# Load order, keys computed ahead and earlier weight sums at the start of a linear-attention and gated-MLP kernel

## The chip, the cores and the metric

One NeuronCore of one Trainium2 chip. The time is the device time of one execution in microseconds (us). Before the change: median 1449.56 us of three runs (1448.41 to 1450.8). TensorE (the matrix engine) is PE in the profiles, VectorE is DVE, ScalarE ACT, GpSimd POOL; a span is the profiled execution from its first to its last instruction.

## The reference, cut to what matters

```python
x = A_x                                   # 1 x 2048 x 1024, bf16
x = x + A(layernorm(x), wqkv, wo)         # linear attention, 32 heads of 32
x = x + B(layernorm(x), w_gate, w_up, w_down)
x = x + A(layernorm(x), wqkv, wo)
x = x + B(layernorm(x), w_gate, w_up, w_down)

def A(x, wqkv, wo):
    q, k, v = split(x @ wqkv)
    pq, pk = phi(q), phi(k)               # phi(t) = where(t > 0, t + 1, exp(t)) + 1e-6
    ...                                   # o = (pq . (pk^T v)) / (pq . sum(pk)), then @ wo
def B(x, ...):  return ((x @ w_gate) * (x @ w_up)) @ w_down
```

## The kernel before

The 2048 tokens are 16 tiles of 128. In the first attention layer a tile is normalised on VectorE and POOL (`start` makes its statistics, `b_one` normalises it), transposed on TensorE and copied by ScalarE (`step_t`), and projected: keys ("k") and queries ("q") in two halves of 512 columns, eight matmuls each. ScalarE and VectorE evacuate each half. Ten tiles are projected plainly. The other token pairs go through "quads", a seven-product scheme for two tiles, which needs sums of weight blocks (`tw_make`, each VectorE instruction over 2048 elements) and of token blocks (`s_make`). The program gives each engine its instructions in a fixed order; a helper adds the semaphores.

```python
NHOLD = 2; NPL1 = 10; LNX = (3, 5, 6)
...
if first:
    lnp.start(0); lnp.b_one()
    lnp.start(1); lnp.step_t(1)
    lnp.b_one();  lnp.start(2)
...
seq = [("k", i) for i in range(NHOLD)] if NPL else []
for i in range(NHOLD, NPL):
    seq += [("q", i - NHOLD), ("k", i)]          # k0 k1 q0 k2 q1 k3 ...
...
for kind, i in seq:
    for h in range(2):
        ev = proj(kind, tok[i], h)               # 8 matmuls
        ev()                                     # exp, relu, min, add
        if kind == "k":
            lnstep(i, h)                         # statistics, normalise; transpose
    if kind == "q" and i >= 1 and len(twk) > 1:
        twk.pop(0)()                             # one weight sum of the keys
    elif kind == "q" and i >= 1 and len(twq) > 1:
        twq.pop(0)()                             # one of the queries
...
for f in twk: f()                                # the last key sum, then the quads
```

The loads are issued in program order on one queue: tile 0, first half of the key weights, tile 1, second half, tile 2, and so on.

Of the kernel before, what the change touches and what calls it, by code (L numbers as in the profile page):

```python
# [180 lines left out]
def build_kernel(nc, A_x, A_wqkv, A_wo, B_w_gate, B_w_up, B_w_down, out):  # L181
    _, S, D = A_x.shape
    F = B_w_gate.shape[1]
    NST, NSB, KT, NG, NFT, NDH = S // 128, S // 512, D // 128, D // 128, F // 128, D // 512
# [8 lines left out]
    NHOLD = 2  # L193
# [128 lines left out]
    with ExitStack() as es:  # L322
# [85 lines left out]
        def r_x(i, lo=0, hi=D):  # L408
            return [(O_X + (i * D + lo) * 2, O_X + (i * D + hi) * 2)]
# [10 lines left out]
        def r_w(base, lo, hi):  # L420
            return _seg(base, KT, D * 2, lo * 2, hi * 2)

        def dma(dst_ap, src_ap, wr, key, rd=()):
            P.add("sp", lambda e: e.dma_start(dst_ap, src_ap), rd=rd, wr=wr, dma_sem=key)
# [218 lines left out]
        def load_w(n, c):  # L643
            t, v, c0, base = WSRC[n]
            dma(t[:, :, c * 512:(c + 1) * 512], v[:, :, c0 + c * 512:c0 + (c + 1) * 512], r_w(base, c * 512, (c + 1) * 512), KW[n][c])
# [28 lines left out]
        def tw_make(n, eng, parts):  # L674
            b11, b12, b21, b22 = [w_blk(n, kb, h) for kb in range(2) for h in range(2)]
            t1, t2, t3, t4 = [tw_blk(n, c) for c in (1, 2, 3, 4)]
            step = 4 // parts
            ops = []
            for o, a, b in ((t1, b12, b11), (t2, b22, t1), (t4, b21, t2), (t3, b22, b12)):
                for k in range(0, 4, step):  # L680
                    def one(o=o, a=a, b=b, k=k):
                        P.add(eng, lambda e: e.tensor_tensor(out=o[0][:, k:k + step], in0=a[0][:, k:k + step], in1=b[0][:, k:k + step], op=ALU.subtract),
                              rd=rsub(a[1], k, step) + rsub(b[1], k, step), wr=rsub(o[1], k, step))
                    ops.append(one)
            return ops
# [33 lines left out]
        def pack():  # L719
            u = pk_n[0]  # L720
            if u >= NU:
                return
            pk_n[0] += 1
            assert RG.get("n", 0) <= u, (RG["n"], u)
            j, m = unit_jm(u)
            w16 = wscr[u].bitcast(BF16)[:, 0:2048].rearrange("p (i k c) -> p i k c", i=2, c=128)
            for i in range(2):
                c0 = j * 256 + (1 - i) * 128
                dma(w16[:, i], wgu_v[m][:, :, c0:c0 + 128], R(V_PK + u * 64 + 32 * i, 32), KPK[u])
# [124 lines left out]
        def s_make(tok, p):  # L854
            a11, a12 = x_blk(tok[2 * p], 0), x_blk(tok[2 * p], 1)
            a21, a22 = x_blk(tok[2 * p + 1], 0), x_blk(tok[2 * p + 1], 1)
            s1, s2, s3, s4 = [s_blk(tok, p, c) for c in (1, 2, 3, 4)]
            return [(lambda o=o, x=x, y=y, op=op: tt(o[0], x[0], y[0], op, x[1] + y[1], o[1]))
                    for o, x, y, op in ((s1, a21, a22, ALU.add), (s2, s1, a11, ALU.subtract),
                                        (s3, a11, a21, ALU.subtract), (s4, a12, s2, ALU.subtract))]  # L860

        def layer_A(lnp, nxt, first):
# [21 lines left out]
            def proj(kind, i, h):  # L884
                t, v, c0, base = WSRC[kind]
                bank = B_KQ[kq_i[0] % len(B_KQ)]
                kq_i[0] += 1

                def fn(e):
                    return [e.matmul(psb(bank), xnT[:, k, i * 128:(i + 1) * 128], t[:, k, h * 512:(h + 1) * 512],  # L890
                                     start=(k == 0), stop=(k == KT - 1)) for k in range(KT)]
                P.add("pe", fn, rd=r_xT(i * 128, (i + 1) * 128) + r_w(base, h * 512, (h + 1) * 512), pwr=[bank])

                def ev():
                    phi_evac(bank, *dst_of(kind, i, h))
                    if kind == "k" and tok.index(i) % 2 and h:
                        z_pair(tok.index(i) // 2)
                return ev
# [128 lines left out]
            def lnstep(i, h):  # L1027
                if h == 0:
                    if lnp.n < NST:
                        lnp.start(lnp.n)  # L1030
                    lnp.b_one()
                else:
                    lnp.use_dma = i + 1 >= NPE_T
                    lnp.step_t(1)

            if first:
                lnp.start(0)
                lnp.b_one()
                lnp.start(1)
                lnp.step_t(1)  # L1040
                lnp.b_one()
                lnp.start(2)
            else:
                lnp.use_dma = True
            NPL = NPL1 if first else 0
            rl.update(on=first, o=O_XN[0] if first else O_XRT[tok[NST - 2]])
            twk = []
            if first:
                twk = tw_make("k", "dve", 1)
                twq = tw_make("q", "dve", 1)  # L1050
            seq = [("k", i) for i in range(NHOLD)] if NPL else []
            for i in range(NHOLD, NPL):
                seq += [("q", i - NHOLD), ("k", i)]
            seq += [("q", i) for i in range(max(NPL - NHOLD, 0), NPL if NPL < NST else 0)]
            npack = [0]
            for kind, i in seq:
                for h in range(2):
                    ev = proj(kind, tok[i], h)
                    ev()
                    if kind == "k":  # L1060
                        lnstep(i, h)
                if kind == "q" and i >= 1 and len(twk) > 1:
                    twk.pop(0)()
                elif kind == "q" and i >= 1 and len(twq) > 1:
                    twq.pop(0)()
                if kind == "q" and NPL < NST and i in LNX:
                    for h in range(2):
                        lnstep(NPE_T, h)
                if kind == "q" and i >= NPL - 2:
                    if i == NPL - 2:  # L1070
                        lnp.need(NPL + 1)
                    for f in s_make(tok, NPL // 2)[2 * (i - NPL + 2):][:2]:
                        f()
                if i >= 3 and kind == "k":
                    pack()
# [19 lines left out]
            for n, (kind, p) in enumerate(items):  # L1095
# [10 lines left out]
                if first:  # L1106
                    i = NPL + len(LNX) + n
# [770 lines left out]
        def xload(i):  # L1878
            dma(x_res[:, i, :], x2[i * 128:(i + 1) * 128, :], r_x(i), KX[i])

        load_w("k", 0)
        xload(1)
        load_w("k", 1)
        xload(2)
        load_w("q", 0)
# [7 lines left out]
        lnA = LN("A0", nat)  # L1893
        lnB = LN("B", nat)
        layer_A(lnA, lnB, True)
        lnA = LN("A", alt)
        layer_B(lnB, lnA, True)
        lnB = LN("B", alt)
        layer_A(lnA, lnB, False)
        layer_B(lnB, None, False)  # L1900

# [5 lines left out]
def bass_interleave_layers__linear_attn_block__glu_gated_bilinear__prompt_kernel(  # L1907
    nc, A_x, A_wqkv, A_wo, B_x, B_w_gate, B_w_up, B_w_down, out,
):
    build_kernel(nc, A_x, A_wqkv, A_wo, B_w_gate, B_w_up, B_w_down, out)  # L1910
# [28 lines left out]
```

## Time and profile before

| | kernel before |
|---|---|
| median of 3 runs | 1449.56 us |
| span of the profiled execution | 1449.1 us, clock 1.000 |
| TensorE busy | 1426.2 us (98%) |
| second half projection of tile 0 starts | 10.67 us |
| keys of tile 1 start | 14.65 us |
| first quad / first token product | 82.39 / 112.46 us |
| output projection / gate and up / end | 187.01 / 244.67 / 1449.1 us |

"Token product" is the first matmul behind the quads. The landmarks are starts of matmul groups in the timeline. The lines behind these numbers stand in the prediction.

### The profile page before, as it was taken

How to read it: one execution, taken by the hardware profiler on the slowest of the kernel's cores; microseconds unless marked ns; L12 is line 12 of the kernel's file. 1: busy time of each engine (PE TensorE's matmuls, PEld its weight loads, DVE VectorE, ACT ScalarE, POOL GpSimd, SP SyncE). 2: the span in 40 equal slices, each digit the busy share in tenths (PEclk: the TensorE clock that was granted, in tenths of full speed). 3: DMA queues.
4: the chain of work that ended last, by engine and by line, in shares of the span. 5: the costliest groups of instructions: out<-in, count | busy, mean ns of one | idle time of the engine just before them, and what ended most of it. 6: DMA issues, size and time to landing. Idle time of an engine off the chain costs nothing.

```text
span 1449.1 us, 21876 instructions
## 1 busy us (share of the span) xinstructions
PE 1426.2 (98%) x8186; PEld 787.3 (54%) x8186; DVE 1218.2 (84%) x2376; ACT 665.6 (46%) x1378; POOL 147.2 (10%) x176
## 2 busy tenths in 40 slices
PE   8999998999999999999999999999999999999999
PEld 3444443455545666664554444446666475666547
DVE  6987887999978799988779878778888887888888
ACT  5673245444420266661037823467776004777400
POOL 2212521000010000002010046210000100000000
PEclk9999999999999999999999999999999999999999
DMA  8578977997786777777985166667775866777653
GB/s 261 88 203 225 198 171 155 289 328 266 266 252 215 235 248 260 245 256 264 268 262 145 40 175 151 184 166 263 261 260 191 277 237 231 265 259 257 207 195 119
DMA packets 270459, 320.22 MB, mean 221 GB/s; under 512 B 161936, under 2 KB 212880, under 8 KB 270352
## 3 DMA queue, kind: packets, MB, share of 16 engines
q1 hardware_dynamic: 270352, 318.82, 72.3%
q8 instruction: 64, 1.05, 0.3%
q14 instruction: 43, 0.35, 0.1%
HBM read 236.45 MB, written 73.40 MB: 214 GB/s over the span
## 4 chain that ended last, share of the span: by engine, by line
PE 80%; DVE 11%; DMA 4%; issue 2%; ACT 2%; POOL 1%; SPq 1%; POOLq 0%; DVEq 0%; ACTq 0%
PE ps L1319 27%; PE ps L1400 16%; PE ps L1736 14%; PE ps L919 6%; PE ps L1138 6%; PE ps L1654 5%; DVE arena L765 3%; PE ps L890 3%; DMA arena<-arena 3%; PE ps L1240 2%; DVE arena L451 2%; DVE arena L768 1%; DVE arena L1015 1%; DVE arena L1012 1%; DVE arena L612 1%
## 5 line engine op out<-in xcount | busy, mean ns | idle before, releaser
L765 DVE TENSOR_TENSOR arena<-arena 128x512 f16<-128x512 f16 (+8 forms) x1015 | 497.8, 518 | 61.6 <-ACT arena L1404 33.6
L1319 PE MATMUL ps<-arena 128*128 128x512 f16 x1888 | 457.3, 379 | 2.7 <-ACT ps L1348 2.0
L768 DVE SCALAR_TENSOR_TENSOR arena<-ps,arena 128x512 f16<-128x512 f32 (+3 forms) x545 | 353.6, 664 | 68.7 <-PE ps L1736 26.9
L1400 PE MATMUL ps<-arena 128*128 128x256 f16 x2184 | 287.5, 273 | 2.2 <-DMA arena<-sp_scratch 1.3
L1319 PEld LDWEIGHTS ps<-arena 128*128 128x128 f16 (+1 forms) x1888 | 182.8, 98 | 165.6 <-ACT ps L1348 6.3
L1400 PEld LDWEIGHTS ps<-arena 128*128 128x128 f16 (+1 forms) x2184 | 212.1, 98 | 93.1 <-ACT arena L1404 6.9
L1736 PE MATMUL ps<-arena 128*128 128x512 bf16 (+1 forms) x1120 | 244.7, 379 | 0.0
L1736 PEld LDWEIGHTS ps<-arena 128*128 128x128 f16 x1120 | 109.6, 98 | 130.2
L1324 ACT ACTIVATE arena<-ps 128x512 f32<-128x512 f32 x224 | 133.7, 597 | 82.2 <-PE ps L1319 64.3
L1404 ACT ACTIVATE arena<-ps 128x256 f32<-128x256 f32 x351 | 125.1, 385 | 26.9 <-PE ps L1400 22.0
L919 PE MATMUL ps<-arena 128*128 128x512 f16 (+1 forms) x560 | 123.2, 379 | 2.7 <-ACT arena L926 0.9
L1138 PE MATMUL ps<-arena 128*128 128x512 bf16 x512 | 116.1, 379 | 0.0
L1240 PE MATMUL ps<-arena 128*128 128x512 bf16 x512 | 111.5, 379 | 3.6 <-ACT ps L1234 3.3
L454 POOL TENSOR_SCALAR arena<-arena 128x1 f32<-128x1 f32 x64 | 24.5, 383 | 804.5 <-DVE arena L453 804.5
L1410 ACT COPY ps<-ps 128x256 f32<-128x256 f32 x182 | 66.4, 365 | 75.0 <-DVE arena L768 29.4
L451 DVE BATCH_NORM_STATS2 arena<-arena 128x6 f32<-128x512 bf16 x128 | 88.2, 689 | 13.9 <-DMA arena<-in_A_x_dram 6.6
L1021 POOL TENSOR_TENSOR arena<-arena 128x1024 f16<-128x1024 f32 x32 | 76.4, 2389 | 184.3 <-DVE arena L1019 167.1
L1348 ACT COPY ps<-ps 128x512 f32<-128x512 f32 x112 | 65.4, 584 | 61.4 <-PE ps L1319 50.2
L1682 ACT COPY arena<-ps 128x256 f32<-128x256 f32 x8 | 3.0, 372 | 197.1 <-PE ps L1654 197.1
L919 PEld LDWEIGHTS ps<-arena 128*128 128x128 f16 x560 | 54.0, 98 | 70.9 <-ACT arena L926 5.1
L890 PE MATMUL ps<-arena 128*128 128x512 bf16 x384 | 85.5, 379 | 3.6 <-ACT arena L555 1.6
L1654 PE MATMUL ps<-arena 128*128 128x256 f16 (+1 forms) x784 | 86.8, 273 | 0.5 <-DVE arena L768 0.3
(61 smaller groups left out, 969.8 us busy)
## 6 DMA issues: line engine op xcount, KB each, us to landing
arena<-w_scratch SPq DMA_DIRECT2D x84, 896.0 KB, 4.6
arena<-t_scratch SPq DMA_DIRECT2D x32, 896.0 KB, 5.8
arena<-in_B_w_down_dram SPq DMA_DIRECT2D x24, 896.0 KB, 5.0
arena<-sp_scratch SPq DMA_DIRECT2D x26, 768.0 KB, 4.2
w_scratch<-arena SPq DMA_DIRECT2D x28, 512.0 KB, 6.3
arena<-w_scratch SPq DMA_DIRECT2D x28, 384.0 KB, 5.2
x_scratch<-arena SPq DMA_DIRECT2D x40, 256.0 KB, 7.4
arena<-x_scratch SPq DMA_DIRECT2D x40, 256.0 KB, 5.9
```

The lines of the kernel that those rows point to most:

```text
L765: P.add("dve", lambda e: e.tensor_tensor(out=out, in0=a, in1=b, op=op), rd=rd, wr=wr, prd=prd)
L768: P.add("dve", lambda e: e.scalar_tensor_tensor(out=out, in0=a, scalar=sc, in1=b, op0=ALU.mult, op1=op1), rd=rd, wr=wr, prd=prd)
L890: return [e.matmul(psb(bank), xnT[:, k, i * 128:(i + 1) * 128], t[:, k, h * 512:(h + 1) * 512], start=(k == 0), stop=(k == KT - 1)) for k ...
L919: P.add("pe", lambda e: [e.matmul(psb(bank), a[0][:, k, :], b[0][:, k, :], start=(q in (1, 5) and k == 0), stop=(k == 3), skip_group_check ...
L1138: return [e.matmul(psb(bank), xrt[t][:, jj * 128:(jj + 1) * 128], pk[:, h, t, :], start=(t == tok[0]), stop=(t == tok[NST - 1])) for t in ts]
L1240: return [e.matmul(psb(bank), xnT[:, g, i * 128:(i + 1) * 128], wp[:, g, dh * 512:(dh + 1) * 512], start=(dh == 0 and g == 0), stop=(g == ...
L1319: P.add("pe", lambda e: [e.matmul(psb(bank), w[:, k, :], x[:, k, :], start=(start and k == 0), stop=(k == 3), skip_group_check=True) for k ...
L1324: P.add("act", lambda e: e.activation(t, psb(bank), AF.Copy, scale=SG), prd=[bank], wr=r)
L1400: P.add("pe", lambda e: [e.matmul(psb(bank)[:, 256 * half:256 * half + 256], w[:, k, :], xx[:, k, :], start=(start and k == 0), stop=(k == ...
L1404: P.add("act", lambda e: e.activation(d, src, AF.Copy, scale=sc), prd=[xk], wr=rd_)
L1654: P.add("pe", lambda e: [e.matmul(psb(bank)[:, 256 * half:256 * half + 256], a[:, k, 128 * r:128 * r + 128], b[:, k, :], start=(start and ...
L1736: P.add("pe", lambda e: [e.matmul(psb(bank), hv[:, 7 * hf + k, t * 128:(t + 1) * 128], w[:, k, :], start=(q in "15" and hf == 0 and k == 0 ...
```

## The change

Its intent: feed TensorE sooner at the start, and take weight sums out of a stretch where VectorE is nearly full (busy 35.50 of the 38 us from 44 to 82). It loads tile 1 ahead of the key weights, transposes it behind the first half projection, projects the keys of three tiles before the first queries, and makes six weight sums earlier. The diff, whole but for context lines:

```diff
                 lnp.b_one()
-                lnp.start(2)
...
-            for i in range(NHOLD, NPL):
-                seq += [("q", i - NHOLD), ("k", i)]
-            seq += [("q", i) for i in range(max(NPL - NHOLD, 0), NPL if NPL < NST else 0)]
+            if NPL:
+                seq.append(("k", NHOLD))
+            for i in range(NHOLD + 1, NPL):
+                seq += [("q", i - NHOLD - 1), ("k", i)]
+            seq += [("q", i) for i in range(max(NPL - NHOLD - 1, 0), NPL if NPL < NST else 0)]
+            lead = [[lambda: lnp.start(2), lambda: lnp.step_t(1)], [lambda: lnp.b_one()], [lambda: lnp.step_t(1), lambda: lnp.start(3)],
+                    [lambda: lnp.b_one()], [], [lambda: lnp.step_t(1)], [lambda: lnp.start(4)], [lambda: lnp.b_one(), lambda: lnp.start(5)]]
...
                     ev()
-                    if kind == "k":
+                    if lead:
+                        for f in lead.pop(0):
+                            f()
+                        if i == NHOLD:
+                            twk.pop(0)()
+                    elif kind == "k":
                         lnstep(i, h)
-                if kind == "q" and i >= 1 and len(twk) > 1:
+                if kind == "q" and len(twk) > 1:
                     twk.pop(0)()
...
+        xload(1)
         load_w("k", 0)
-        xload(1)
         load_w("k", 1)
```

## The prediction

> **What bounds the kernel now.** I began with the page's engine totals. TensorE is the bound:
>
> ```profile
> PE 1426.2 (98%) x8186; PEld 787.3 (54%) x8186; DVE 1218.2 (84%) x2376; ACT 665.6 (46%) x1378; POOL 147.2 (10%) x176
> ```
>
> Of a span of 1449.1 us TensorE is idle for 22.9 us. The diff adds and removes no matmul, so it can win only from this idle time, and only where it reaches: the first projections of layer one. I then tabulated busy time by stage (columns: stretch, length, busy us and instructions of PE, PEld, DVE, ACT, POOL, granted clock, DMA share, GB/s):
>
> ```profile
> 0.00:20.00 20.00, 14.43 (x73) 6.43 (x74) 11.00 (x23) 8.20 (x13) 6.00 (x24) 1.00 0.96 316
> 20.00:44.00 24.00, 24.00 (x131) 11.61 (x129) 19.93 (x48) 17.14 (x30) 5.41 (x8) 1.00 0.45 134
> 44.00:82.00 38.00, 37.85 (x177) 16.97 (x175) 35.50 (x81) 22.70 (x43) 10.61 (x16) 1.00 0.68 118
> 82.00:88.00 6.00, 4.93 (x22) 1.78 (x21) 5.83 (x16) 4.15 (x8) 0.00 (x0) 1.00 0.80 295
> 88.00:112.00 24.00, 24.00 (x113) 10.87 (x111) 20.13 (x50) 18.79 (x35) 0.00 (x0) 1.00 0.69 189
> ```
>
> Two holes stand out: 5.6 us of idle PE in the first 20 us, and 1.1 us between 82 and 88, just where VectorE is busy for 5.83 of 6 us. Between them TensorE never stops, though VectorE is 93% full from 44 to 82 (35.50 of 38). The timeline shows what makes the holes (start, duration, engine, line, what it does, idle time before it and releaser):
>
> ```profile
> 7.68 1.42 DVE L451 BATCH_NORM_STATS2 arena<-arena 128x6 f32<-128x512 bf16 x2 [1.45 <-DMA arena<-in_A_x_dram]
> ...
> 10.67 1.90 PE L890 MATMUL ps<-arena 128*128 128x512 bf16 x8 [0.92 <-DMA arena<-in_A_wqkv_dram]
> ...
> 14.65 3.63 PE L890 MATMUL ps<-arena 128*128 128x512 bf16 x16 [1.64 <-ACT arena L555]
> ...
> 83.75 3.00 PE L919 MATMUL ps<-arena 128*128 128x512 f16 x12 [0.33 <-DVE arena L765]
> ...
> 86.06 1.22 DVE L682 TENSOR_TENSOR arena<-arena 128x2048 f16<-128x2048 bf16 x1
> ...
> 87.42 25.20 PE L919 MATMUL ps<-arena 128*128 128x512 f16 x116 [0.68 <-ACT arena L616]
> ```
>
> The statistics of token tile 1 wait for its load until 7.68 us, because the 1 MB first half of the key weights goes ahead of it. Its normalisation ends at 10.90, behind the first half projection on PE; its transpose (12.41) and copy follow, and keys of tile 1 start at 14.65. At 82 to 88 the first quad (the seven-product scheme for two tiles) runs into a late VectorE: its second product waits for a sum, and the last four matmuls start at 87.42, just after the key weight sum of L682 ended at 87.28. I take that sum for the real releaser, as the seventh product reads it, though the profile names an exponential that ended at 87.38. The chain of waits runs from 87.42 to 148 over PE alone.
>
> [...] 1218 ns for each weight sum. [...] tile 1, issued behind 1 MB of key weights, arrives only at 7.7 us, and the second key half, issued next, at 10.62. [...] the trace's 16 matmuls take 3.45 us, 216 ns each, at a granted clock of 1.00.
>
> **The change part by part.**
>
> *Load order.* Ahead of the second key half lie the same bytes as before (tile 0, tile 1, first key half), so it still arrives at about 10.6. Tile 1 now has only tile 0 ahead of it. In the first 12 us the loads run at some 360 GB/s once going, so its 0.26 MB take 0.7 us more than tile 0, which came at 3.0 to 3.8: well before VectorE is free of tile 0 (6.24). The first key half arrives later by the same 0.7 us: counting bytes by microsecond, 6.9 becomes 7.7, still just before the 7.86 at which its matmuls start (that start waits for a ScalarE copy). So this costs nothing.
>
> *Tile 1 earlier.* Its statistics run from 6.24 to 7.66, aggregate and the two POOL steps take 1.3 us, the normalisation 0.5: ready at about 9.5 instead of 10.90. The transpose (0.45 to 0.6 us) now stands after the first half projection, at 9.77, in the gap in which PE waits for weights until 10.67. Its copy (1.02) follows two evacuations on ScalarE (0.60 and 0.49) and ends at 11.9. Keys of tile 1 follow the second half of tile 0 directly: 10.67 + 1.90 = 12.57 instead of 14.65, a gain of 2.08.
>
> *Keys of tile 2 before queries of tile 0.* Tile 2 still arrives at 11.33 (same bytes ahead). Statistics until 12.9, POOL until 14.0, then normalisation behind one evacuation: 14.6. PE finishes the first half of tile 1 at 14.30, so it waits some 0.35 for the transpose of tile 2. Halves then start at 15.1 and 16.83; before, the same work had reached that point at 18.57. Gain so far 1.74.
>
> *Weight sums.* Eight sums of 1.22 us exist in both kernels. Before, six lie at 31.1, 38.5, 45.8, 55.0, 60.8 and 70.0, three of them in the full stretch. After, three of the key sums come with tile 2 and query 0 and three query sums with queries 1 to 3, done by about 50. Following VectorE item by item with durations from the trace (evacuation 0.66, start of a tile's statistics 1.57, normalisation 0.41, pair sum 0.7 or 1.4, weight sum 1.15) it falls behind PE by 5 to 6 us between 30 and 55 and then catches up: it does the last query of the stretch right after PE, which now ends at 82.39 - 1.74 = 80.65. Of the 5.03 us between 82.39 and 87.42, 16 matmuls need 3.46, so 1.57 can be won if nothing waits. The last key sum, which overwrites weights of the last key projection, then lies near 82.8 to 84.0, just when the seventh product wants it (80.65 + 3.46 = 84.1).
>
> *Sum.* 1.74 + 1.57 = 3.3 us at 87.42. From there the code is the same; until 148 the chain is pure PE, then normalisations on VectorE, DMA transposes and PE again, all released by earlier work of this program and not by a clock, so I carry the gain one for one: 1449.56 - 3.3 = 1446.3.
>
> **Rivals.**
>
> 1. *VectorE lateness stalls PE.* The statistics for tiles 3 to 5 and the sums all move forward, into 14 to 30 us. Against it: there are four PSUM banks, and two buffers for the rectified part, so PE needs the VectorE addition of a half only about six halves (10 us) later; my worst lag is 6 us. The tightest case is the transpose of tile 4, normalised at about 26.7 and wanted by PE at 27.7 to 28. If it slips by 2 us the first gain is gone: 1448.3 or so.
>
> 2. *The gain is absorbed later.* DMA is full where the normalisations run (share about 1.07 from 150 to 180), and PE idles 6.8 us from 148 to 260. If those transfers started at fixed times the gain would vanish: 1449.5. For: a DMA transpose takes 6.39 us on the chain at 171. Against: nearly all of them are issued behind work that also moves; the only free-running queue, tiles and first copies of the gate weights, is empty by 30 us. I expect up to 1 us lost or won by transfers meeting differently.
>
> 3. *Only the load order and first transposes pay,* the quad's hole staying, because the last key sum is still late or ScalarE is: 1449.56 - 1.7 = 1447.8.
>
> 4. *The first key half comes late.* More than 0.4 us after 7.86 would push the second half behind 10.67. The queue rate speaks against it; it would cost under 1 us.
>
> **Range and chances.** The best sum, with no wait for tile 2's transpose, is 2.08 + 1.57 = 3.65, to which up to 1 us of luck in the transfers may come: 1444.5 or so. The worst likely is rival 1 or most of rival 2: about 1448.8. Three runs before spread over 2.4 us. Two per cent is 29 us, more than all of PE's idle time, so faster by over 2% is impossible by this mechanism, and slower by over 2% would need a stall of 29 us that no wait here suggests. Within 2%: 0.98.
>
> **What would show each step.** In the changed profile: the first statistics of tile 1 near 6.2 without a wait for the load; a transpose in PE's gap before 10.7; key matmuls of tile 1 at 12.6, not 14.65, with a gap of about 0.3 near 14.5; no weight sums of 2048 elements between 52 and 80 and six before; the first quad's matmuls starting near 80.7 and its long continuous run near 84.1, not 87.42; matmul counts unchanged and PE's idle time about 19.6. The prediction is wrong if idle time of PE appears between 16 and 80, if the last key sum ends after 85.5, or if the shift at 148 is 3 us and at 260 is not.

The measured values: 1218 ns for a weight sum, arrivals at 7.7 and 10.62 us, 216 ns for a matmul of 512 columns. That what is issued first arrives first was the assumption: the trace shows these two arrivals, and the forecast that the second key half still comes at about 10.6 is an estimate from them. The sum came to 1.74 + 1.57 = 3.3 us, so 1446.3. The "four PSUM banks" are those that this kernel gives to the key and query projections (`B_KQ`).

## The result, and the profile after

1447.6 us median of four runs (1447.51 to 1449.19), against 1449.26 for the kernel before with one more run. Ratios here are the mean time of one kernel's fast runs over that of the other's of the same rounds, so not quite the ratio of the quoted medians: 0.999, interval 0.9973 to 1.0007. The time lies in the predicted range, but the gain, 1.7 us by the medians, is half of the 3.3 forecast. More runs of the same kernel later gave 0.9983 (0.9969 to 0.9997).

The page's totals of the profile after (profiled time 1449.19, span 1447.5):

```profile
PE 1424.8 (98%) x8125; PEld 788.2 (54%) x8186; DVE 1217.8 (84%) x2376; ACT 666.7 (46%) x1378; POOL 147.0 (10%) x176
```

61 matmul records are missing (8125 against 8186, while the weight loads are all there), so busy time can't settle whether PE's idle time fell. The stages, with the columns of the prediction's table, do:

```profile
0.00:20.00 20.00, 15.28 (x73) 6.71 (x75) 10.22 (x23) 8.61 (x13) 5.57 (x24) 0.91 0.96 313
20.00:44.00 24.00, 23.84 (x128) 11.62 (x129) 22.56 (x49) 16.84 (x29) 5.53 (x8) 1.00 0.49 143
44.00:82.00 38.00, 37.84 (x175) 17.21 (x176) 35.87 (x87) 24.24 (x44) 10.63 (x16) 1.00 0.67 154
82.00:88.00 6.00, 5.91 (x27) 2.39 (x26) 5.00 (x10) 4.25 (x8) 0.00 (x0) 1.00 0.30 109
```

Both things aimed at are there. VectorE works 2.6 us more between 20 and 44 (22.56 against 19.93), and the hole at 82 to 88 is closed (PE 5.91 of 6, was 4.93). Between 44 and 82 VectorE is no emptier than before (35.87 against 35.50): with the sums gone it does later work sooner, and the last key sum starts at 84.27 instead of 86.06. But the granted clock of the first 20 us is 0.91; before it was 1.00. The timeline shows what that did:

```profile
6.10 1.41 DVE L451 BATCH_NORM_STATS2 arena<-arena 128x6 f32<-128x512 bf16 x2
...
7.88 3.40 PE L890 MATMUL ps<-arena 128*128 128x512 bf16 x8 [1.02 <-ACT arena L547]
...
11.12 0.61 PE L553 MATMUL ps<-arena 128*128 128x128 f16 x8
...
11.56 3.48 PE L890 MATMUL ps<-arena 128*128 128x512 bf16 x15
...
16.19 0.62 PE L553 MATMUL ps<-arena 128*128 128x128 f16 x8 [1.14 <-DVE arena L471]
```

The statistics of tile 1 no longer wait for a load and the transpose of tile 1 follows the first half projection, as planned. But that half projection took 3.40 us, not 1.90: half the speed. The transpose behind it started at 11.12 instead of the forecast 9.77. The second half projection started at 11.56, though its weights had landed at about 11.0, and tile 2's transpose then waited 1.14 us, which cost another 0.56 (70.31 against 69.75 in the table below). So of the 1.5 us some 1.1 were left at the first quad. Microsecond by microsecond the clock (the third number from the end) shows one block at a half:

```profile
7.00:8.00 1.00, 0.12 (x1) 0.14 (x2) 0.73 (x2) 0.75 (x2) 0.15 (x1) 0.78 1.07 350
8.00:9.00 1.00, 1.00 (x3) 0.30 (x2) 0.24 (x1) 0.00 (x0) 0.65 (x2) 0.50 1.09 365
9.00:10.00 1.00, 1.00 (x4) 0.33 (x3) 0.31 (x1) 0.00 (x0) 0.00 (x0) 0.50 1.10 356
10.00:11.00 1.00, 1.00 (x4) 0.42 (x3) 0.00 (x0) 0.00 (x0) 0.00 (x0) 0.52 1.04 363
11.00:12.00 1.00, 1.00 (x13) 0.65 (x11) 0.06 (x1) 0.68 (x2) 0.00 (x0) 1.00 1.10 356
```

A second such block lies behind PE's wait at the start of the gate and up projections. First the kernel before, then after, the same 20 matmuls:

```profile
248.54 4.49 PE L1319 MATMUL ps<-arena 128*128 128x512 f16 x20 [1.98 <-ACT ps L1348]
```

```profile
245.31 6.18 PE L1327 MATMUL ps<-arena 128*128 128x512 f16 x20 [1.99 <-ACT ps L1356]
```

And the clock of the kernel after in that stretch:

```profile
246.00:248.00 2.00, 2.00 (x7) 0.72 (x6) 1.97 (x6) 0.60 (x1) 0.00 (x0) 0.62 0.32 126
248.00:250.00 2.00, 2.00 (x6) 0.76 (x5) 1.86 (x5) 0.00 (x0) 0.00 (x0) 0.52 0.94 221
```

Another 1.69 us. The matmuls started 3.23 us earlier than before (245.31 against 248.54) and ended 1.54 us earlier: half of a gain of 3.2 us was lost in this one block.

Read in steps of a quarter and a half us, the two stretches of half clock (0.50) lie at 7.56 to 10.97 and 246.49 to 249.90, both 3.41 us long. What sets such a stretch off, the traces do not show. So my theory: the mechanism gives about 3.3 us, and what is missing was taken by half-clock blocks, which come at these places in some executions and not in others. Rivals: the gain is absorbed downstream whatever the clock; the half clock belongs to this change; a single part pays and the rest does nothing. (A "filler" below is a group of matmuls whose results are thrown away, put into a wait of PE to see whether the granted clock then stays at 1.00.)

### The profile page after: what moved, and what is told of

It reads as the page before. It is cut to its first block, busy times and chain, and to the rows that moved or that the text cites. A ratio compares the mean times of both kernels' runs of the same rounds, so it can differ in the third digit from the quotient of the medians.

```text
span 1447.5 us, 21815 instructions
## 1 busy us (share of the span) xinstructions
PE 1424.8 (98%) x8125; PEld 788.2 (54%) x8186; DVE 1217.8 (84%) x2376; ACT 666.7 (46%) x1378; POOL 147.0 (10%) x176
## 4 chain that ended last, share of the span: by engine, by line
PE 83%; DVE 10%; DMA 2%; issue 2%; POOL 2%; ACT 1%; SPq 0%; POOLq 0%; DVEq 0%; ACTq 0%
PE ps L1327 28%; PE ps L1408 16%; PE ps L1744 14%; PE ps L919 6%; PE ps L1146 6%; PE ps L890 5%; PE ps L1662 5%; DVE arena L765 3%; PE ps L1248 2%; DVE arena L451 2%; DMA arena<-arena 1%; DVE arena L1015 1%; DVE arena L1012 1%; DVE arena L768 1%; POOL arena L1021 1%
## 5 line engine op out<-in xcount | busy, mean ns | idle before, releaser
L765 DVE TENSOR_TENSOR arena<-arena 128x512 f16<-128x512 f16 (+9 forms) x1015 | 497.7, 518 | 60.5 <-ACT arena L1412 33.6
```

What stands on the lines that cost most here:

```text
L765: P.add("dve", lambda e: e.tensor_tensor(out=out, in0=a, in1=b, op=op), rd=rd, wr=wr, prd=prd)
```

## The experiments

Every output was correct. Five rounds each, at most four kernels together on one chip, sharing runs of the kernel before. Twelve kernels in all.

**1. The changed kernel again** (no edit).

> The changed kernel once more. Clock theory: the 3.3 us of the mechanism are there[...]; so this profile shows other stretches or none, and the key matmuls of tile 1 start at 12.6 if none lies at 7.9, at about 13.3 if one does. Without any stretch a time near 1446.0; over several runs a spread of some 1.5 to 3 us, in both kernels. Rival (the gain is absorbed downstream): the half clock at 7.9 and 246 is no cause, a profile without it is as long, 1447.5. Rival (half clock belongs to the change): the same two stretches appear again at the same places.

Measured: median 1447.68 (1445.26 to 1450.39), ratio to before 0.9983. The profile (span 1446.3) has no block in front:

```profile
8.03 1.89 PE L890 MATMUL ps<-arena 128*128 128x512 bf16 x8 [1.13 <-DMA arena<-in_A_wqkv_dram]
9.75 0.61 PE L553 MATMUL ps<-arena 128*128 128x128 f16 x8
10.97 3.41 PE L890 MATMUL ps<-arena 128*128 128x512 bf16 x15 [0.62 <-DMA arena<-in_A_wqkv_dram]
15.04 0.62 PE L553 MATMUL ps<-arena 128*128 128x128 f16 x8 [0.66 <-DVE arena L471]
```

This is the predicted schedule: the transpose fills PE's gap, keys of tile 1 follow the second half at once, tile 2's transpose waits a little. The first quad started at 80.72 (predicted 80.65). The block behind 244 appeared again (20 matmuls in 6.18 us). So the front block is not a fixed part of the change. The profiled time, 1448.07, and the scatter, 5.1 us, were above the forecast. Over all ten runs of the changed kernel, the two with a mean clock of 1.000 average 1446.4 us (they lie 2.3 us apart), the eight below it 1448.42. Of the 30 runs of the kernel before whose clock is recorded, 13 were at 1.000 (mean 1449.38) and 17 below (1450.73); but the difference is 2.85 us in the first set of rounds and nothing in the last (1449.76 and 1449.78).

**2. Clock held in front.** The filler goes into PE's wait between the first transposes and the first projection:

```diff
-    PE_WARM = 10
+    PE_WARM = 11
...
                 lnp.step_t(1)
+                P.add("pe", lambda e: [e.matmul(psb(B_KVT[1]), wrm[:, 0:128], wrm, start=True, stop=True) for _ in range(5)], ...)
                 lnp.b_one()
```

> The changed kernel with one more warm-up matmul and five matmuls on zeros in PE's gap between the first transposes (end 6.65) and the first key matmuls (7.88), results thrown away. Clock theory: [...]the granted clock is 1.00 from 7 us on, keys of tile 1 start at 12.6, the wait for tile 2's transpose is at most 0.4, the first quad starts at 80.4 to 80.7, and the first 112 us are 1.5 us shorter than in the profile after; time 1446.0 to 1446.5 if no stretch lies at 246. Rival: no shorter than the changed kernel (1447.6).

Measured: 1446.95 (1445.79 to 1447.99), ratio 0.9975; clock 1.00 in every stretch of the front; four of five runs at 1.000. Against the changed kernel in the same rounds the mean is 1.2 us lower (1446.85 against 1448.05), less than those runs scatter. The first quad started late, at 81.40, because the second key half came late here (second half projection at 11.65); counted from that, it is as in run 1 (69.75 us). So the forecast that the first 112 us would be 1.5 us shorter was missed: the token product started at 110.20 against 110.67.

**3. Load order alone**, in the kernel before:

```diff
+        xload(1)
         load_w("k", 0)
-        xload(1)
```

> The kernel before with nothing but the load of tile 1 ahead of the key weights. My theory: the statistics of tile 1 start at 6.1 instead of 7.7, but PE takes the transpose only after both halves of tile 0, and ScalarE copies it after their evacuations, so keys of tile 1 still start at 14.65: same time as before, within 0.3 us, first quad at 82.4. Rival (the load order is the gain): keys of tile 1 at 12.6 to 13.5, 1 to 2 us faster.

Measured: 1450.92 (1448.41 to 1452.35), ratio 1.0: no gain. The landmarks I had expected were missed: the first key half came only at 9.16 and the clock was at a half from about 8.2 to 15.0, so the first quad began at 85.46.

**4. Everything but the load order**: run 3's edit taken back in the changed kernel.

> The changed kernel with the loads in the old order. My theory: the normalisation of tile 1 ends at 10.9, its transpose follows at once and holds the second half of tile 0 back from 10.67 to about 11.35; keys of tile 1 start at about 13.1, the transpose of tile 2 at about 15.1: some 0.5 us behind the changed kernel without a half-clock stretch (with one at 7.9, equal to it), the quad's gain stays. So 0.3 to 0.6 us slower than the changed kernel at the same clock. Rival (load order is what pays): as slow as the kernel before up to 16 us.

Measured: 1448.14 (1446.34 to 1451.07), ratio 0.998, as the changed kernel in the same rounds (0.9983). This profile too had a half clock in front (10 to 16.9) and late key weights (9.11, in the old load order), so its landmarks say little; run 11 repeats it.

**5. The filler in the kernel before.**

> The kernel before with the same filler matmuls as after_warm (one more warm-up, five behind the first transposes), so that both orders can be compared with the clock granted in front. My theory: keys of tile 1 start 1.64 us after the second key half's results are taken, at 14.65 plus whatever the key weights come later in this execution (the filler ends at 8.1, so at most 0.3 by itself); first quad 67.7 us after that; the quad's hole of 1.6 us stays. after_warm is then 3.3 us faster than before_warm (ratio 0.9977), and before_warm is at most 1 us faster than the kernel before. Rival (warming is what helped in after_warm): before_warm gains as much over the kernel before as after_warm, 2 us or more, and the two differ by under 1.5 us.

Its profiled execution took 8574.94 us and is left out as slow: records of 512-column matmuls lasted 1705 ns on the mean instead of 379, and they followed each other every 1.33 us (33 in 43.95 us) instead of 216 ns, through the whole kernel, with VectorE at its usual speed (292 ns for L612, 298 in the kernel before). The recorded clock was 1.000; what set this off is not known. The other four: 1448.21 to 1452.09, ratio 1.0005. So warming in front shows no gain in the kernel before; the rival (warming is the gain) falls.

**6. Weight sums alone moved forward**, with the front filler, in the old order:

```diff
+                    if kind == "k" and i == NHOLD:
+                        twk.pop(0)()
-                if kind == "q" and i >= 1 and len(twk) > 1:
+                if kind == "q" and len(twk) > 1:
```

> before_warm with nothing but the weight sums moved forward (key sums with query 0 and the keys of tile 2, query sums with queries 1 to 3). My theory: front as in before_warm, keys of tile 1 at the same time; the 3.66 us of VectorE work taken out of the stretch 45 to 82 let VectorE keep up, and the first quad runs through: from its first matmul to the first token-product matmul 28.8 us instead of 30.1; 1.3 us faster than before_warm (ratio to the kernel before 0.999). Rival (the sums lie beside other work anyway): same as before_warm, 30.1 us in the quads.

Measured: 1448.89 (1447.63 to 1450.01), ratio 0.9992. VectorE between 44 and 82 fell to 34.75 us (35.50 before), PE in 82 to 88 rose to 5.91, and the quads took 28.80 us instead of 30.07. The forecast of 1.3 us for the hole holds; the time agrees in size but is not clear of noise.

**7. The change with the sums left late**, with the front filler (the diff of run 6, backwards).

> after_warm with the weight sums at their old places. My theory: the front gain of about 2 us stays (keys of tile 1 right behind tile 0), the quad's hole comes back, quads 30.1 us instead of 28.8; 1.3 to 1.6 us slower than after_warm, 1.7 us faster than before_warm. Rival (the early start of PE alone gives VectorE the room): as fast as after_warm, quads 28.8 us.

Measured: 1448.17 (1447.72 to 1449.84), ratio 0.9991, 1.7 us above run 2 by the means (of other rounds, and with one run of five at clock 1.000 against four, so this is not the sums alone). The quads took 29.56 us: the hole comes back, but only by 0.76 us, not 1.3; that VectorE gains from the earlier start as well would explain it, but no run separates this. Both sides were half right.

**8. Second filler**: eight thrown-away matmuls in PE's 1.99 us wait before the gate and up projections:

```diff
                     P.add("act", lambda e: e.copy(psb(Z[c]), psb(X[c])), prd=[X[c]], pwr=[Z[c]])
+                    if jit and p == 0 and c == 1:
+                        P.add("pe", lambda e: [e.matmul(psb(B_L2[0]), ident, T1.rearrange("p k s -> p (k s)")[:, 0:512], start=True, stop=True) for _ in range(8)], ...)
```

> after_warm with eight more thrown-away matmuls in PE's wait of 1.99 us at the start of the gate and up projections (242 to 245). Clock theory: the granted clock stays 1.00 from 240 to 260 in this profile, the executions that lost 1.7 us there no longer do; median 0.3 to 1 us below after_warm and a smaller spread. Rival: the half clock there never cost time in the end: no difference from after_warm (within 0.5 us), or slower if the filler holds back the next matmuls.

Measured: 1446.88 (1446.19 to 1447.41), ratio 0.9979; clock 1.000 in all five runs. The median is only 0.1 below run 2, so the lower bound of the forecast was missed; the spread is smaller, 1.2 us.

**9 to 12. The decisive set, with both fillers**: before, load order alone, all but the load order, and the change, in the same rounds on one chip. The edits are those above.

> The kernel before with both fillers of after_warm2: the comparison with after_warm2_b at a granted clock of 1.00. My theory, counted from the start of the second half projection of tile 0 (the arrival of the second key half): first quad after 71.7 us, first token-product matmul after 101.8 us, as in the profile before; against 98.55 in the changed order, so 3.2 us there. In the time: clock 1.00 in nearly all executions, about 1449.0, after_warm2_b 2 to 3 us faster (ratio of the two about 0.998). Rival (the gain does not survive downstream): under 1 us between the two.

> before_warm2 with the load of tile 1 ahead of the key weights. My theory: no gain, because PE takes the transpose of tile 1 after both halves of tile 0 in any case: 101.8 us from the second half projection to the first token product, time within 0.5 us of before_warm2; if the new load order delays the key weights, as the arrivals so far hint (second half started at 10.5 and 10.7 in the old order, 10.9 to 11.7 in the new one), it is 0.3 to 1 us slower. Rival (load order is the gain): 1 to 2 us faster than before_warm2.

> after_warm2 with the loads in the old order. My theory: the transpose of tile 1, normalised at 10.9, stands ahead of the second half projection and starts it near 11.4 to 11.5, later than the key weights alone (10.6) would; then keys of tile 1 follow at once and tile 2's transpose waits about 0.5; first quad 69.75 to 70.2 us after the second half projection: so about as fast as after_warm2_b, within 0.6 us. Rival (the two parts need each other): 1 us or more slower than after_warm2_b.

> after_warm2 unchanged, in the same rounds as the other three. Clock 1.00 in nearly all executions, first token product 98.55 us after the second half projection, 1204.4 us from the first gate and up matmul to the end; time 1446.9, 2 to 3 us faster than before_warm2. Rival: as before_warm2 says.

All 20 runs had a clock of 1.000. Ratios are to the kernel before without fillers, in the same rounds.

| with both fillers | median (range) us | mean us | ratio to the kernel before |
|---|---|---|---|
| 9 before | 1449.75 (1449.41 to 1449.82) | 1449.65 | 1.0 |
| 10 load order alone | 1449.53 (1448.59 to 1450.56) | 1449.58 | 0.9998 |
| 11 all but load order | 1447.07 (1445.89 to 1447.72) | 1447.01 | 0.9982 |
| 12 the change | 1446.29 (1445.06 to 1447.21) | 1446.17 | 0.9976 (0.9964 to 0.9989) |

At full clock the change gains 1449.65 - 1446.17 = 3.5 us (2 to 3 were expected). The load order alone gains nothing. With the rest it goes with another 0.8 us, between the 0.6 of my theory and the 1 of the rival and less than the scatter of the runs (1.8 and 2.2 us), so the times alone do not show it; PE's timeline shows where it would lie. First load order alone (run 10), then all but load order (run 11), then the change (run 12):

```profile
11.21 1.90 PE L890 MATMUL ps<-arena 128*128 128x512 bf16 x8 [1.02 <-DMA arena<-in_A_wqkv_dram]
12.94 0.61 PE L553 MATMUL ps<-arena 128*128 128x128 f16 x8
```

```profile
11.59 0.62 PE L553 MATMUL ps<-arena 128*128 128x128 f16 x8 [1.45 <-DVE arena L471]
12.05 3.62 PE L890 MATMUL ps<-arena 128*128 128x512 bf16 x16
```

```profile
10.13 0.61 PE L553 MATMUL ps<-arena 128*128 128x128 f16 x8
11.34 3.63 PE L890 MATMUL ps<-arena 128*128 128x512 bf16 x16 [0.60 <-DMA arena<-in_A_wqkv_dram]
```

In run 10 the transpose of tile 1 stands behind both halves, so that an early tile is of no use. In run 11 the transpose is in the right place but waits 1.45 us for VectorE, and pushes the second half projection to 12.05. In run 12 it fits the gap, and the second half starts when its weights arrive, 0.7 us earlier, although the weights landed at about 11.3 in both. The quads of run 12 then run through, where the kernel before stopped twice (83.75 and 87.42 in the prediction):

```profile
81.09 28.96 PE L919 MATMUL ps<-arena 128*128 128x512 bf16 x132
```

The profiles, cut at the landmarks (S is the start of the second half projection; differences in us):

| profile | S | S to first quad | quads | token product to output projection | to gate and up | to the end |
|---|---|---|---|---|---|---|
| before | 10.67 | 71.72 | 30.07 | 74.55 | 57.66 | 1204.43 |
| 9 before, fillers | 10.84 | 71.72 | 30.07 | 73.28 | 57.63 | 1204.56 |
| 10 load order | 11.21 | 71.72 | 30.07 | 73.25 | 57.73 | 1204.82 |
| 6 sums | 10.49 | 71.39 | 28.80 | 73.55 | 57.43 | 1204.44 |
| 7 change, late sums | 10.91 | 69.75 | 29.56 | 73.69 | 57.82 | 1204.67 |
| 11 all but load order | 12.05 | 69.73 | 28.80 | 72.86 | 57.66 | 1204.20 |
| after | 11.56 | 70.31 | 28.80 | 73.53 | 57.23 | 1206.07 |
| 1 after again | 10.97 | 69.75 | 28.80 | 73.06 | 57.63 | 1206.09 |
| 12 change, fillers | 11.34 | 69.75 | 28.80 | 72.61 | 57.75 | 1204.55 |

From S to the token product the change takes 98.55 us at full clock, the kernel before 101.79: a gain of 3.24, of which sums alone give 1.60 and the change with late sums 2.48 (they share 0.84). The last column shows the block behind 244 in the two profiles without the second filler that had one: 1206.1 against 1204.2 to 1204.8. The middle column wanders by 1.9 us among these rows without a pattern that the edits explain; in the profiles of runs 3 and 4, whose front was 3 us late, it was shortest (71.97 and 71.98), so that stage can take up some lateness. How it does so stays open. In runs 9 and 12 it adds 0.67 us to the gain (73.28 against 72.61), about what the later S of run 12 takes away (0.50); that the end shows 3.3, as forecast, is in that part luck.

## Why the prediction was right or wrong, point by point

- **The bound and the two holes**: right. In the kernel before with fillers PE was busy 4.93 of the 6 us at 82, with the change 5.97.
- **Tile 1 earlier, keys of tile 2 ahead**: right. The forecast gain of 1.74 us at the first quad, counted from S, was 1.97 (71.72 to 69.75). The wait for tile 2's transpose was 0.44 us in the filled kernels with the whole change and 0.66 in run 1 instead of 0.35.
- **Weight sums**: right in kind, 0.3 too large. The hole of 1.57 us gave back 1.27 (30.07 to 28.80). The prediction counts three sums in the full stretch; its own list has four (45.8 to 70.0), of which one stays (50.7).
- **"So this costs nothing"** (load order and key weights): no cost is shown. At first I counted from the second half projection: 11.29 us on the mean of six profiles with the new load order against 10.67 of three with the old. But this leaves out runs 4 and 11, old order too, where the transpose hides the arrival. Issue time plus time to landing of the second key half gives 10.4, 10.6, 10.8, 11.3 and 12.7 in the five profiles with the old order and 10.8 to 12.0 in the eight with the new: means of 11.2 and 11.3. What failed is the fixed arrival "at about 10.6": it scatters by some 2 us in either order. The first key half scatters too: it landed at 6.9 in the kernel before, and in run 4, in the same load order, PE waited for it until 9.11. Why is open.
- **Rival 1** (VectorE stalls PE between 16 and 80): refuted. In runs 1 and 12 PE waits for nothing there; in the profile after only tile 2's transpose, behind the half clock, does.
- **Rival 2** (absorbed later): refuted at full clock; 2.74 us at the token product (112.63 to 109.89, runs 9 and 12) were 3.3 at the end of the same two executions and 3.5 in the means.
- **Rival 3** (the hole stays): refuted by the quads, 28.80 us instead of 30.07.
- **Rival 4** (first key half late): it came true without its cost. The first key half landed at 7.8 to 9.1 us in the eight profiles with the new order (forecast 7.7), and in five of them the first projection started more than 0.4 after 7.86; at full clock the second half projection still waited only for its own weights.
- **The range**: its low end, "1444.5 or so", is 0.4 below its own sum (1449.56 - 3.65 - 1 = 1444.9). The measured 1447.6 lay inside.
- **The step that failed**: I took the clock as granted, "216 ns each, at a granted clock of 1.00", and carried the gain on that assumption. In eight of ten runs of the changed kernel the mean clock was below 1.000, and these were 2.0 us slower than the other two (1448.42 against 1446.40, close to the forecast 1446.3). In the profile after, the two blocks cost 1.5 and 1.69 us where they lay, of which some 1.1 and 1.6 lasted: its gain was 1.79 us at the token product, 3.24 at gate and up (1.45 of it from the two stretches between, which no edit touches) and 1.60 at the end. That clock blocks are the main reason why 1447.6 and not 1446.3 was measured is shown for the profiled execution and supported by the grouping; that each run lost its time there is not shown, because only one execution of each kernel has its profile here.
- **What sets a block off** is not shown. The wait before gate and up is 1.98 or 1.99 us in every profile without the second filler but that of run 5. In the profiles after and run 1 half clock followed it (246.49 to 249.90, and from about 244.6 to 248.0), and the 20 matmuls behind it took 6.18 us; in the kernel before and in runs 2, 3, 4, 6 and 7 they took 4.49. In front, the block of the profile after came behind waits of PE of 1.19 and 1.02 us; run 1, with a wait of 1.13 us there, had none. So the same wait cost 1.7 us or nothing, and its length alone does not decide.
- **Open**: whether the change makes half-clock blocks likelier (8 of 10 against 17 of 30 is too little to say), and why the fillers brought the kernel before no gain (ratios 1.0 and 1.0005) though its runs below full clock were 1.35 us slower over all rounds; in the rounds of run 9 they were not slower, so there was nothing to win.

The change with both fillers is the fastest measured: 1446.29 and 1446.88 in two sets, with no run above 1447.41.

## What to carry to other kernels

Where a start-up chain passes through several engines in program order, an earlier load paid here only together with an earlier place of its consumer on every engine behind it: alone it gave nothing (mean 1449.58 us against 1449.65), and without it the moved transpose stood waiting for 1.45 us. A few microseconds at the start are worth no more than the clock at which they run (here the same eight matmuls took 1.90 us at a granted clock of 1.00 and 3.40 at 0.50): look at the granted clock microsecond by microsecond, and try thrown-away matmuls in short waits of TensorE ahead of dense work (here all 25 runs with both fillers were at full clock and the changed kernel scattered less; its gain of 1.2 us with the first was not clear of noise, and the kernel before gained nothing). Take arrival times from the landing of the transfer itself, since a consumer that waits for something else hides a late arrival, and count stages from one landmark to the next; then a 3 us gain can be read from a few traces although runs scatter by as much.
